# Seven products over 1280 rows, y with w1 w_out among them, in float16

## The chip, the core and the metric

The kernel runs on one core of one Trainium2 chip. The metric is the device time of one execution in microseconds (us). The median before is 390.21 us over four runs (389.89, 390.18, 390.24 and 396.35). The profile was taken on the execution of 390.18 us.

## The reference

A gated recurrence over 4 sequences of 6144 tokens with 256 channels, and then a two-layer network over all 24576 tokens, whose hidden value is the larger of two products.

```python
def _attn_ref(x, f_logit, lower_bound):          # x, f_logit: (4, 6144, 256)
    sig = 1.0 / (1.0 + np.exp(-f_logit))
    f = lower_bound + (1.0 - lower_bound) * sig
    i = 1.0 - f
    for t in range(S):
        h = f[:, t] * h + i[:, t] * x[:, t]
        y[:, t] = h
...
def _moe_ref(x, w1, w2, w_out):                  # x: (24576, 256); w1, w2: (256, 1024); w_out: (1024, 256)
    h1 = x @ w1
    h2 = x @ w2
    g = np.maximum(h1, h2)
    return g @ w_out
```

The kernel uses max(h1, h2) = h1 + relu(h2 - h1). So the output is y (w1 w_out) + relu(y (w2 - w1)) w_out: the first layer is one product, with `wd` = w2 - w1, and its output `r` is evicted through Relu; the matrix `w13` = w1 w_out (256 by 256) takes y straight to the output. Both carry the factor 1 - lower_bound, which the recurrence leaves out.

## The kernel before, in words

**Tiles.** A block is 512 tokens of one sequence (48 blocks), a pair is two blocks, `ja` and `jb` (24 pairs, numbered from 0). Channels and hidden units lie on the partitions, tokens along the free dimension. Blocks 0 to 3 are worked off by a prologue, in which also the weights are made. From pair 2 on a pair is one chunk of 1024 tokens, number c = pair + 2: its f_logit and x are cast to 16 bits into a DRAM scratch by the software queue of GpSimd (`fetch`, L96) and turned by two transposing DMAs of SyncE (`cross`, L144) into tiles `fT` and `xT`. There are two scratch tiles for each input, so GpSimd waits (`pool_waits`, L344) for the transposes of a chunk before it fetches the chunk after the next.

**Recurrence.** ScalarE makes u = sigmoid(-f) in four ACTIVATEs of a pair (`pair_gate`, L272); VectorE makes `ff` and `v` and runs four scans of 512 tokens (`pair_scans`, L285). Their outputs are the tiles `y`.

**First layer.** `first_layer(j, fc)` (L424 on) makes 128 hidden units of a block with two matmuls of 512 columns, into half of a PSUM tile `dT`. After each second call ScalarE evicts both halves through Relu into `r` (L440). There are two `dT` tiles.

**Second layer.** The hidden units of a pair of blocks are four quarters, r of `ja` and `jb` by k = 0 (the first 512) and k = 1. The output has two column halves, `lo` and `hi`. A two by two by two product by Winograd's variant of Strassen's scheme needs seven products of blocks in place of eight; the two rows are `ja` and `jb`. Its left sums S1 to S4 (`sum1` to `sum4`, L507 on) are made on VectorE for each pair, its right sums `t1` to `t4` once (`make_sevens`, L399). `sevenths(p)` (L519) lists the matmuls of one pair, each 128 by 128 by 128: a product is four token tiles times four rows of 128 hidden units. Beside the seven products stand four `linear` groups, which add y times w13 (L531): four token tiles times two channel halves each. The sums run in three PSUM banks: X is carried through five of the products, E through two and B through one. Where a partial sum is needed twice, `snapshot` copies it to SBUF (`sn`, ScalarE, L556). `leave` (L560) brings a bank out into `osb`: by a VectorE add of a snapshot (L568) or by a ScalarE copy (L566), and issues the store when a block is complete.

**The order of the work** is written out by hand (`manual_schedule`). The main loop runs over the pairs p = 2 to 23, each in 16 slots. A slot is one `first_layer` call of pair p and a sixteenth of the second layer of pair p - 1. VectorE's work for p + 1, the sums and ScalarE's gates are put at slots by the lists `seq` and `gates`. In p = 2 the slots carry the plain second layer of block 3. The last two blocks get their second layer after the loop, in plain form (`second_layer`, L461 on).

Slot s of the loop takes the entries of `seq` with a number below 9 (s + 1). Each engine works off its own instructions in the order in which they are written.

Of the kernel before, what the change touches and what calls it, by code (L numbers as in the profile page):

```python
# [10 lines left out]
BF16 = mybir.dt.bfloat16  # L11
# [7 lines left out]
def kernel(  # L19
# [19 lines left out]
    HC = 4  # L39
# [17 lines left out]
    def by_xbar(c, s):  # L57
# [13 lines left out]
    ypool = ctx.enter_context(tc.tile_pool(name="ypool", bufs=7))  # L71
    rpool = ctx.enter_context(tc.tile_pool(name="rpool", bufs=10))
# [12 lines left out]
        [dram.tile([CH, D], BF16, name=f"scr{s}{q}") for q in range(NSCR)]  # L85
# [10 lines left out]
    def fetch(c, s):  # L96
        b, t0, nt, _ = chunks[c]
        src = srcs[s][b, t0 : t0 + nt, :]
        if by_xbar(c, s):
            nc.gpsimd.dma_start(  # L100
                out=pieces(scratch[s][c % NSCR][:]), in_=pieces(src)
            )
        else:
            nat = inpool.tile([P, TB // P, D], BF16, name=("fT", "xT")[s])
            nc.gpsimd.dma_start(
                out=nat[:].rearrange("p i d -> p (i d)"),
                in_=src.rearrange("(p i) d -> p (i d)", p=P),
            )
            held[c, s] = nat
# [15 lines left out]
    def first_bf16(k, s, copy):  # L125
        raw = raws[k, s]
        nat = const.tile([P, TB // 2 // P, D], BF16, name=f"nat{k}{s}")
        copy(out=nat[:], in_=raw[:])
        raws[k, s] = nat

    def first_turn(k):
        nt = TB // 2
        for s in range(2):
            dst = ps_o.tile([P, KC, nt // P, P], BF16, name="ps")
            for q in range(nt // P):
                for h in range(KC):
                    nc.tensor.transpose(
                        dst[:, h, q, :],
                        raws[k, s][:, q, h * P : (h + 1) * P],
                        ident[:],  # L140
                    )
            raws[k, s] = dst[:].rearrange("p k i m -> p k m i")

    def cross(cs, after):  # L144
# [6 lines left out]
        for c in cs:  # L151
            for s in range(2):
                dst = inpool.tile([P, KC, CH], BF16, name=("fT", "xT")[s])
# [9 lines left out]
    def turn_steps(j):  # L163
        b, t0, nb, c, o = blocks[j]
        steps = []
        for s in range(2):
            dst = ps_o.tile([P, KC, TB], BF16, name="ps")
# [16 lines left out]
    ys = {}  # L184
    mids = {}

# [5 lines left out]
    def new_mid(key, names):  # L192
        for t in names:
            mids[key, t] = midpool.tile([P, KC, CH], BF16, name=t)
# [26 lines left out]
    def scan(j, h, ff, v, o):  # L221
        b, t0, nb, _, _ = blocks[j]
        nc.vector.tensor_tensor_scan(  # L223
            out=ys[j][:, h, :],
            data0=ff[:, h, o : o + TB],
            data1=v[:, h, o : o + TB],
            initial=0.0 if t0 == 0 else ys[j - 1][:, h, TB - 1 : TB],
# [4 lines left out]
    def scan_steps(j):  # L232
        new_mid(j, ("ff", "v"))
        u, ff, v = (mids[j, t] for t in ("u", "ff", "v"))
        ys[j] = ypool.tile([P, KC, TB], BF16, name="y")
# [7 lines left out]
    def first_recurrence(k):  # L243
        nt = TB // 2
        cols = slice(k * nt, (k + 1) * nt)
        if k == 0:
            new_mid(0, ("u", "ff", "v"))
            ys[0] = ypool.tile([P, KC, TB], BF16, name="y")
        u, ff, v, y = (*(mids[0, t] for t in ("u", "ff", "v")), ys[0])
# [6 lines left out]
        for h in range(KC):  # L256
            nc.vector.tensor_tensor_scan(
                out=y[:, h, cols],
                data0=ff[:, h, cols],
                data1=v[:, h, cols],  # L260
                initial=y[:, h, nt - 1 : nt] if k else 0.0,
# [23 lines left out]
    def pair_scans(p):  # L285
# [3 lines left out]
        for j in (2 * p, 2 * p + 1):  # L289
            ys[j] = ypool.tile([P, KC, TB], BF16, name="y")  # L290
# [19 lines left out]
    ident = const.tile([P, P], BF16)  # L310
# [3 lines left out]
    seen = const.tile([1, 16], BF16)  # L314
    waited = const.tile([P, 1], FP32)
    warm = const.tile([P, 1], FP32)
    wob = wpool.tile([P, FC, D], BF16)
    wd = wpool.tile([P, KC, DFF], BF16)
    w1T = wpool.tile([P, FC, D], BF16)
    w13 = wpool.tile([P, KC, D], BF16)  # L320
    w13d = wpool.tile([P, KC, P], BF16)
    t1 = wpool.tile([P, HC, P], BF16)
    t2 = wpool.tile([P, HC, P], BF16)
    t3 = wpool.tile([P, HC, P], BF16)
    t4 = wpool.tile([P, HC, P], BF16)
    wcd = wpool.tile([P, FC, P], BF16, name="wcd") if HC < KH else None
# [71 lines left out]

    def make_sevens():  # L399
        b11, b12 = wob[:, 0:HC, lo], wob[:, 0:HC, hi]  # L400
        b21, b22 = wob[:, KH : KH + HC, lo], wob[:, KH : KH + HC, hi]

        def minus(out, a, b):
            return lambda: nc.vector.tensor_tensor(
                out=out, in0=a, in1=b, op=ALU.subtract
            )

        steps = [
            minus(t1[:], b12, b11),
            minus(t3[:], b22, b12),  # L410
            minus(t2[:], b22, t1[:]),
            minus(t4[:], b21, t2[:]),
            minus(w13d[:], w13[:, :, lo], w13[:, :, hi]),
        ]
        if wcd is not None:
            steps.append(minus(wcd[:], wob[:, :, lo], wob[:, :, hi]))
        return steps


    rts = {}  # L420
    dts = {}

    def first_layer(j, fc):
        y = ys[j]  # L424
# [3 lines left out]
        if g == 0:  # L428
            rts[j, k] = rpool.tile([P, KH, TB], BF16, name="r")
        dT = dts["d"]  # L430
        for kc in range(KC):
# [3 lines left out]
                rhs=y[:, kc, :],  # L435
# [24 lines left out]
    def second_layer(j, slot):  # L460
        ns = TB // P  # L461
        y = ys[j]
        n = KC + FC
        total = ns * n
        for k in range(slot * total // FC, (slot + 1) * total // FC):
# [8 lines left out]
            if s < KC:  # L474
                left, right = y[:, s, i:TB:ns], w13[:, s, :]
# [23 lines left out]
    def sum_of(p, name, a, b, op):  # L499
        t = spool.tile([P, HC, TB], BF16, name="S")  # L500
# [3 lines left out]
    def quarter(p, t, k):  # L504
        return rts[2 * p + t, k][:, 0:HC, :]
# [13 lines left out]
    def sevenths(p):  # L519
# [5 lines left out]
        def product(b, left, right, fresh=False):  # L525
            n = HC
            for i in range(TB // P):
                for k in range(n):
                    steps.append([b, left, right(k), i, k, fresh and i == k == 0, None])

        def linear(b, j, cols, diff):  # L531
            y = ys[j]
            ops = [
                (y[:, kc, :].rearrange("p (m i) -> p i m", m=P), w13d[:, kc, :] if diff else w13[:, kc, cols])
                for kc in range(KC)
            ]
            for k in range(2):
                for g in range(HC, KH):
                    fc = k * KH + g
                    ops.append(  # L540
                        (
                            rts[j, k][:, g, :].rearrange("p (i m) -> p i m", m=P),
                            wcd[:, fc, :] if diff else wob[:, fc, cols],
                        )
                    )
            for i in range(TB // P):
                for a, w in ops:
                    steps.append([b, a, w, i, None, False, None])

        def then(fn):  # L550
            steps[-1][-1] = fn

# [22 lines left out]
        def sub(n):  # L575
            return lambda k: sums[p, n][:, k, :]

        def part(t, k2):
            return lambda k: rts[2 * p + t, k2][:, k, :]

        product("X", part(0, 0), lambda k: wob[:, k, lo], True)
        then(snapshot("X", 1))
        product("B", part(0, 1), lambda k: wob[:, KH + k, lo], True)
        linear("B", ja, lo, False)
        then(leave("B", ja, lo, 1, False))
        product("X", sub(2), lambda k: t2[:, k, :])
        then(snapshot("X", 2))
        product("E", sub(1), lambda k: t1[:, k, :], True)
        then(snapshot("E", 5))
        product("X", sub(3), lambda k: t3[:, k, :])  # L590
        linear("X", jb, hi, False)
        then(leave("X", jb, hi, 5, False))
        product("E", sub(4), lambda k: wob[:, KH + k, hi])
        linear("E", ja, hi, False)
        then(leave("E", ja, hi, 2, True))
        product("X", part(1, 1), lambda k: t4[:, k, :])
        linear("X", jb, lo, True)
        then(leave("X", jb, lo, None, True))

        def runner(step):  # L600
            b, left, w, i, k, fresh, after = step

            def run():
                if fresh:
                    bank[b] = ps_o.tile([P, TB // P, P], FP32, name="ps")
                if k is None:
                    a = left[:, i, :]
                else:
                    a = left(k)[:, i * P : (i + 1) * P]
                nc.tensor.matmul(  # L610
                    bank[b][:, i, :],
                    lhsT=a,
# [11 lines left out]
    with tc.manual_schedule():  # L624
# [19 lines left out]
        wt = ps_d.tile([P, 2, 2 * TB], BF16, name="dT")  # L644
# [68 lines left out]

        for p in range(PAIR0, NPAIR):
# [3 lines left out]
            if more:  # L718
                scans = pair_scans(p + 1)
                seq += [  # L720
                    (10, scans["drive0"]),
                    (44, scans["decay"]),
                    (46, scans["scan00"]),
                    (66, scans["scan01"]),
                    (76, scans["drive1"]),
                    (84, scans["scan10"]),
                    (104, scans["scan11"]),
                    (124, lambda: sum3(p)),
                ]
            if not first:  # L730
                seq += [
                    (0, lambda: sum2(p - 1)),
                    (20, lambda: sum1(p - 1)),
                    (56, lambda: sum4(p - 1)),
                ]
            seq.sort(key=lambda e: e[0])
            steps = [] if first else sevenths(p - 1)
            done_steps = 0
            gates = {2: (1, 2), 4: (1, 3), 13: (2, 0), 15: (2, 1)}
            for slot in range(2 * FC):  # L740
                first_layer(2 * p + slot // FC, slot % FC)
                if first:
                    if slot % 2 == 0:
                        second_layer(2 * p - 1, slot // 2)
                upto = (slot + 1) * len(steps) // (2 * FC)
                for step in steps[done_steps:upto]:
                    step()
                done_steps = upto
                if slot in gates:
                    q, n = gates[slot]  # L750
                    if p + q < NPAIR:
                        pair_gate(p + q, n)
                while seq and seq[0][0] < (slot + 1) * 9:
                    seq.pop(0)[1]()
                if slot == 2 and p + 3 < NPAIR:
                    c = blocks[2 * p + 6][3]
                    cross((c,), (c + 1, c + 2) if first else (c + 2,))
        for j in (NBLK - 2, NBLK - 1):
# [32 lines left out]
```

## Time and profile before

| | |
|---|---|
| profiled execution | 390.18 us, of which the program's span is 388.4 us |
| TensorE matmul (PE) | busy 370.6 us (95%), 4064 instructions seen |
| VectorE (DVE) | busy 320.8 us (83%), 383 |
| ScalarE (ACT) | busy 290.0 us (75%), 383 |
| GpSimd (POOL) | busy 50.4 us (13%), 100 |
| granted TensorE clock | 9 tenths or more in all 40 slices, 0.998 in the mean |
| chain that ended last | PE 84%, DMA 6%, DVE 4%, ACT 2% |
| DMA queues | 77.17 MB; the hardware queue of SyncE takes 61.0% of sixteen engines' span, the software queue of GpSimd 31.9% |

A group row of the page names the line, the engine, the operation, the tiles (output <- inputs), the shape and the count, then the busy time in us and the mean of one in ns, then the engine's idle time before and what ended it. Two neighbouring instructions of an engine overlap a little in the records, so a duration is longer than the time from one start to the next. Matmuls are pipelined: their row means (219 ns for 128 columns, 381 ns for 512) hold the latency too; the time that one takes from the engine is read from the distance of starts.

### The profile page before, as it was taken

How to read it: one execution, taken by the hardware profiler on the slowest of the kernel's cores; microseconds unless marked ns; L12 is line 12 of the kernel's file. 1: busy time of each engine (PE TensorE's matmuls, PEld its weight loads, DVE VectorE, ACT ScalarE, POOL GpSimd, SP SyncE). 2: the span in 40 equal slices, each digit the busy share in tenths (PEclk: the TensorE clock that was granted, in tenths of full speed). 3: DMA queues.
4: the chain of work that ended last, by engine and by line, in shares of the span. 5: the costliest groups of instructions: out<-in, count | busy, mean ns of one | idle time of the engine just before them, and what ended most of it. 6: DMA issues, size and time to landing. Idle time of an engine off the chain costs nothing.

```text
span 388.4 us, 9544 instructions
## 1 busy us (share of the span) xinstructions
PE 370.6 (95%) x4064; PEld 278.4 (72%) x4136; DVE 320.8 (83%) x383; ACT 290.0 (75%) x383; POOL 50.4 (13%) x100
## 2 busy tenths in 40 slices
PE   3999999998999999999999999999999999999995
PEld 2576667776777777777777777777777777777784
DVE  4977599995998988989989989989989889889521
ACT  3645888776788797797797787887887977977740
POOL 1500102301021021111102001202230201000000
PEclk9999999999999999999999999999999999999999
DMA  7996998989999999999999999999999994220222
GB/s 251 231 232 122 247 179 204 218 174 216 221 258 269 107 279 272 204 193 300 189 148 207 249 197 272 257 194 263 267 231 216 259 191 82 110 111 2 110 107 111
DMA packets 103389, 77.17 MB, mean 199 GB/s; under 512 B 93554, under 2 KB 94066, under 8 KB 102642
## 3 DMA queue, kind: packets, MB, share of 16 engines
q1 hardware_dynamic: 100514, 51.13, 61.0%
q0 software_dynamic: 2544, 25.17, 31.9%
q8 instruction: 32, 0.52, 0.6%
q10 hardware_dynamic: 288, 0.26, 0.2%
q14 instruction: 11, 0.09, 0.1%
HBM read 53.48 MB, written 48.23 MB: 262 GB/s over the span
## 4 chain that ended last, share of the span: by engine, by line
PE 84%; DMA 6%; DVE 4%; ACT 2%; issue 2%; SPq 1%; ACTq 0%
PE ps L610 40%; PE dT L432 35%; PE ps L479 6%; DMA fT<-scr 4%; ACT r L440 2%; DMA r<-in_moe_w_dram 2%; DVE y L223 1%; DVE S L501 1%; PE ps L373 1%; PE ps L182 1%; DVE osb L568 1%; DVE v L216 0%; ACT u L278 0%; PE ps L386 0%; SPq L117 0%
## 5 line engine op out<-in xcount | busy, mean ns | idle before, releaser
L440 ACT ACTIVATE r<-dT 128x1024 bf16<-128x1024 f32 x192 | 196.9, 1027 | 70.3 <-PE dT L432 69.4
L432 PE MATMUL dT<-y,wd 128*128 128x512 bf16 x696 | 210.7, 381 | 4.3 <-ACT r L440 2.2
L610 PEld LDWEIGHTS <-S 128*128 128x128 bf16 x1344 | 89.2, 98 | 34.7
L223 DVE TENSOR_TENSOR_SCAN y<-ff,y,v 128x512 bf16<-128x512 bf16 x88 | 112.0, 1278 | 0.8
L610 PEld LDWEIGHTS <-r 128*128 128x128 bf16 x1008 | 66.9, 98 | 27.9 <-issue 0.7
L610 PE MATMUL ps<-t,S 128*128 128x128 bf16 x1008 | 76.8, 219 | 0.5
L432 PEld LDWEIGHTS <-wd 128*128 128x128 bf16 x768 | 61.5, 98 | 11.8 <-issue 4.6
L501 DVE TENSOR_TENSOR S<-r,S 128x2048 bf16<-128x2048 bf16 x42 | 50.9, 1212 | 15.3 <-ACT r L440 15.1
L568 DVE TENSOR_TENSOR osb<-ps,sn 128x512 f32<-128x512 f32 x63 | 42.5, 675 | 23.4 <-ACT r L440 21.5
L610 PEld LDWEIGHTS <-y 128*128 128x128 bf16 x672 | 49.6, 114 | 16.4
L278 ACT ACTIVATE u<-fT 128x512 bf16<-128x512 bf16 x88 | 56.6, 644 | 3.9 <-DMA fT<-scr 3.8
L610 PE MATMUL ps<-wob,r 128*128 128x128 bf16 x672 | 51.2, 219 | 0.5
L501 DVE TENSOR_TENSOR S<-r 128x2048 bf16<-128x2048 bf16 x42 | 51.1, 1216 | 0.0
L610 PE MATMUL ps<-w,y 128*128 128x128 bf16 x504 | 48.7, 219 | 0.4
L345 POOL CAST waited<-fT 128x1 f32<-128x1 bf16 x21 | 12.7, 603 | 199.4 <-DMA fT<-scr 199.4
L556 ACT COPY sn<-ps 128x512 f32<-128x512 f32 x63 | 37.1, 589 | 0.4
L216 DVE TENSOR_TENSOR v<-u,xT 128x1024 bf16<-128x1024 bf16 x44 | 29.7, 675 | 6.7 <-ACT u L278 5.2
L610 PE MATMUL ps<-t,r 128*128 128x128 bf16 x336 | 29.0, 219 | 0.6 <-DVE osb L568 0.3
L610 PE MATMUL ps<-wob,S 128*128 128x128 bf16 x336 | 29.0, 219 | 0.2
L479 PE MATMUL ps<-wob,r 128*128 128x256 bf16 x192 | 26.2, 273 | 0.1
L206 DVE TENSOR_SCALAR ff<-u,nom 128x1024 bf16<-128x1024 bf16 (+2 forms) x54 | 22.0, 448 | 4.5 <-ACT u L200 3.9
L479 PEld LDWEIGHTS <-r 128*128 128x128 bf16 x192 | 18.8, 98 | 3.6
(53 smaller groups left out, 144.5 us busy)
## 6 DMA issues: line engine op xcount, KB each, us to landing
out_dram<-osb SPq DMA_DIRECT2D x47, 512.0 KB, 4.4
scr<-in_f_logit_dram POOLq DMA_DIRECT2D x22, 512.0 KB, 7.5
scr<-in_x_dram POOLq DMA_DIRECT2D x22, 512.0 KB, 9.8
r<-in_moe_w_dram SPq DMA_DIRECT2D x4, 512.0 KB, 7.2
fT<-in_f_logit_dram POOLq DMA_DIRECT2D x3, 256.0 KB, 8.7
xT<-in_x_dram POOLq DMA_DIRECT2D x3, 256.0 KB, 9.4
osb<-in_f_logit_dram SPq DMA_DIRECT2D x2, 256.0 KB, 3.7
osb<-in_x_dram SPq DMA_DIRECT2D x2, 256.0 KB, 3.9
```

The costliest lines, as they stand in the source:

```text
L206: nc.vector.tensor_scalar(out=ff[:, h, cols], in0=u[:, h, cols], scalar1=nom[:, h : h + 1], scalar2=1.0, op0=ALU.mult, op1=ALU.add,)
L216: nc.vector.tensor_tensor(out=like(v[:, :, cols], xT), in0=like(u[:, :, cols], xT), in1=xT, op=ALU.mult,)
L223: nc.vector.tensor_tensor_scan(out=ys[j][:, h, :], data0=ff[:, h, o : o + TB], data1=v[:, h, o : o + TB], initial=0.0 if t0 == 0 else ys[j ...
L278: nc.scalar.activation(out=mids[p + NBLK, "u"][:, h, cols], in_=held[c, 0][:, h, cols], func=AF.Sigmoid, scale=-1.0,)
L345: nc.gpsimd.tensor_copy(out=waited[:], in_=t)
L432: nc.tensor.matmul(dT[:, fc % 2, :], lhsT=wd[:, kc, fc * P : (fc + 1) * P], rhs=y[:, kc, :], start=(kc == 0), stop=(kc == KC - 1),)
L440: nc.scalar.activation(out=rts[j, k][:, g - 1 : g + 1, :].rearrange("p q (i m) -> p q i m", m=P), in_=dT[:].rearrange("p q (m i) -> p q i ...
L479: nc.tensor.matmul(ps[:, r, :], lhsT=left, rhs=right, start=(s == 0 and (r == 0 or j == NBLK - 1)), stop=(s == n - 1 and (r == 1 or j == N ...
L501: nc.vector.tensor_tensor(out=t[:], in0=a, in1=b, op=op)
L556: nc.scalar.copy(out=t[:], in_=bank[b][:])
L568: nc.vector.tensor_tensor(out=dst, in0=bank[b][:], in1=snap[name][:], op=ALU.add)
L610: nc.tensor.matmul(bank[b][:, i, :], lhsT=a, rhs=w, start=fresh, stop=after is not None, skip_group_check=True,)
```

## The change

All 16-bit tiles become float16 where they were bfloat16. The tile `y` is gone: an `r` tile gets a fifth row of 512 tokens, in which the scan writes y (channel half k beside the hidden units of half k). With that the inner dimension of each quarter is 640 rows, four rows of r and one of y, and w13 is the fifth row of the right side. The `linear` groups and `w13d` go; each product is four token tiles times five rows; the sums S run over five rows. `seed` is new: when X holds its first product, ScalarE copies bank X into bank B in PSUM, and the product of B adds to that. B then leaves by a ScalarE copy and no longer by a VectorE add. The products come in another order. The matmuls of the pairs' second layers stand in one queue, from which each slot takes 8.75 in the mean, beginning at slot 2 of p = 3; so a pair's second layer ends in slot 1 of the iteration after the next. What is left in the queue after the loop is issued before the last two blocks. The entries of `seq` and `gates` and the place of `cross` within a slot move.

```diff
-BF16 = mybir.dt.bfloat16
+HALF = mybir.dt.float16
...
-    HC = 4
+    LAG = 2
+    NSEV = 7 * 4 * 5
...
-    ypool = ctx.enter_context(tc.tile_pool(name="ypool", bufs=7))
-    rpool = ctx.enter_context(tc.tile_pool(name="rpool", bufs=10))
+    rpool = ctx.enter_context(tc.tile_pool(name="rpool", bufs=12))
...
+    def new_block(j):
+        for k in range(KC):
+            rts[j, k] = rpool.tile([P, KH + 1, TB], HALF, name="r")
+
+    def y_of(j, k):
+        return rts[j, k][:, KH, :]
...
+    def right(k, cols):
+
+        return wob[:, k * KH : (k + 1) * KH, cols], w13[:, k, cols]
...
     def sum_of(p, name, a, b, op):
-        t = spool.tile([P, HC, TB], BF16, name="S")
+        t = spool.tile([P, KH + 1, TB], HALF, name="S")
...
     def quarter(p, t, k):
-        return rts[2 * p + t, k][:, 0:HC, :]
+        return rts[2 * p + t, k][:]
...
+        def seed(b, src):
+            def go():
+                open_bank(b)
+                nc.scalar.copy(out=bank[b][:], in_=bank[src][:])
+            return go
...
-        product("X", part(0, 0), lambda k: wob[:, k, lo], True)
-        then(snapshot("X", 1))
-        product("B", part(0, 1), lambda k: wob[:, KH + k, lo], True)
-        linear("B", ja, lo, False)
-        then(leave("B", ja, lo, 1, False))
-        product("X", sub(2), lambda k: t2[:, k, :])
-        then(snapshot("X", 2))
-        product("E", sub(1), lambda k: t1[:, k, :], True)
-        then(snapshot("E", 5))
-        product("X", sub(3), lambda k: t3[:, k, :])
-        linear("X", jb, hi, False)
+        product("X", part(0, 0), plain(0, lo), True)
+        then(seed("B", "X"))
+        product("E", sub(1), given(t1), True)
+        then(snapshot("E", 5))
+        product("X", sub(2), given(t2))
+        then(snapshot("X", 2))
+        product("B", part(0, 1), plain(1, lo))
+        then(leave("B", ja, lo, None, False))
+        product("X", sub(3), given(t3))
         then(leave("X", jb, hi, 5, False))
-        product("E", sub(4), lambda k: wob[:, KH + k, hi])
-        linear("E", ja, hi, False)
+        product("E", sub(4), plain(1, hi))
         then(leave("E", ja, hi, 2, True))
-        product("X", part(1, 1), lambda k: t4[:, k, :])
-        linear("X", jb, lo, True)
+        product("X", part(1, 1), given(t4))
         then(leave("X", jb, lo, None, True))
...
-                    (10, scans["drive0"]),
-                    (44, scans["decay"]),
-                    (46, scans["scan00"]),
-                    (66, scans["scan01"]),
-                    (76, scans["drive1"]),
-                    (84, scans["scan10"]),
-                    (104, scans["scan11"]),
+                    (28, scans["drive0"]),
+                    (46, scans["decay"]),
+                    (48, scans["scan00"]),
+                    (68, scans["scan01"]),
+                    (80, scans["drive1"]),
+                    (88, scans["scan10"]),
+                    (108, scans["scan11"]),
                     (124, lambda: sum3(p)),
...
-                    (0, lambda: sum2(p - 1)),
-                    (20, lambda: sum1(p - 1)),
-                    (56, lambda: sum4(p - 1)),
+                    (9, lambda: sum1(p - 1)),
+                    (18, lambda: sum2(p - 1)),
+                    (58, lambda: sum4(p - 1)),
                 ]
+                queue += sevenths(p - 1)
...
-            gates = {2: (1, 2), 4: (1, 3), 13: (2, 0), 15: (2, 1)}
+            gates = {0: (1, 2), 2: (1, 3), 13: (2, 0), 15: (2, 1)}
...
-                upto = (slot + 1) * len(steps) // (2 * FC)
-                for step in steps[done_steps:upto]:
-                    step()
+                if p > PAIR0 + 1 or (p == PAIR0 + 1 and slot >= LAG):
+                    due += NSEV / (2 * FC)
+                    while due >= 1:
+                        due -= 1
+                        queue.pop(0)()
...
+        for step in queue:
+            step()
```

## The prediction

> **What bounds the kernel.** I cut the span into stretches of 15 us first (columns: length, then busy us and count of PE, PEld, DVE, ACT, POOL, then clock, DMA share, GB/s). From 105 to 375 us they are alike:
>
> ```profile
> 180.00:195.00 15.00, 14.84 (x178) 11.27 (x179) 13.36 (x16) 12.14 (x17) 1.90 (x4) 1.00 1.13 226
> ```
>
> PE is busy 14.84 of 15.00 us at full clock, VectorE 13.36, ScalarE 12.14. Does anything hold PE up? The chain of waits there consists of PE alone:
>
> ```profile
> 180.69 0.50 PE ps L610 x9
> 181.20 0.43 PE dT L432 x2
> 181.63 0.50 PE ps L610 x9
> ```
>
> So a slot is two wide matmuls (0.43 us, 215 ns each) and nine narrow ones (0.50 us, 56 ns each). The loop is **bound by PE's instruction count**. The list of waits shows exceptions (total, times, longest):
>
> ```profile
> ACT r L440 <- PE dT L432: 69.4, 135, 4.2
> ...
> ACT u L278 <- DMA fT<-scr: 3.8, 2, 3.0
> ...
> PE dT L432 <- ACT r L440: 2.2, 4, 1.5
> ```
>
> ScalarE has slack, but two transposes come late. The timeline has the second:
>
> ```profile
> 91.28 0.63 ACT L278 ACTIVATE u<-fT 128x512 bf16<-128x512 bf16 x1 [3.04 <-DMA fT<-scr]
> ...
> 92.87 0.59 PE L432 MATMUL dT<-y,wd 128*128 128x512 bf16 x2 [1.45 <-ACT r L440]
> ```
>
> The gate of slot 13, p = 4, stands in ScalarE's queue ahead of slot 15's relu. It waits for chunk 8, and at slot 2 of p = 5 both dT tiles are full, so PE stands until 92.87. What chunk 8 waits for is DMA work all the way back: transposes at 33.8, 53.0, 66.6 and 80.2 us, each after the fetch that GpSimd issued when the chunk before had landed. No step of that chain waits for PE. **Whatever PE gains before 92.87 is lost there.**
>
> From 92.87 to the first plain second-layer matmul at 375.34 lie 302 slots (14 of p = 5, 18 x 16): 282.47 / 302 = 0.935 us a slot, as the pieces say.
>
> **The change part by part.**
>
> *Products of 640 rows.* Before, a pair has 7 x 16 + 32 = 144 narrow matmuls (21 pairs: 3024); after, 7 x 20 = 140. A slot loses 0.25 of one: 302 x 0.25 x 56 ns = **4.2 us less**. The strided weight loads of y take 114 ns against 98; that costs nothing now, since eight matmuls on y run at the same 56 ns (slot of 88.94 us), and they become fewer (28 a pair for 32). A rule to set against this row: the Trainium skill, "TensorE: Matmul & The Clock Gate", Back-to-back issue gap, gives load-and-multiply pairs about 81 ns at 128 columns and 131 ns at 512. By it a slot would last 0.99 us and the saving be 302 x 0.25 x 81 = 6.1 us. The trace has 56 and 215 ns, so I keep 4.2.
>
> *The lag.* In p = 3 the slots 0 and 1 carry no second layer. PE stands for slot 15's relu before slot 2 then anyway (until 60.86), so nothing is gained. The 8.75 of 334 slots make 2922 of 2940; 18 matmuls come after the loop: 18 x 56 ns = **1.0 us more**.
>
> *VectorE.* The rows for its costs:
>
> ```profile
> L501 DVE TENSOR_TENSOR S<-r 128x2048 bf16<-128x2048 bf16 x42 | 51.1, 1216 | 0.0
> L568 DVE TENSOR_TENSOR osb<-ps,sn 128x512 f32<-128x512 f32 x63 | 42.5, 675 | 23.4 <-ACT r L440 21.5
> L556 ACT COPY sn<-ps 128x512 f32<-128x512 f32 x63 | 37.1, 589 | 0.4
> ```
>
> The same operation on 512 elements takes 406 ns (L404), so 512 elements more cost (1216 - 406) / 3 = 270 ns: a sum takes 1.49 us, four 1.08 us more. One add of three goes: 0.6 us less, start to start. By starts (a sum 1.13, a scan 1.13 to 1.20) a pair is about 13.1 us of VectorE before and **13.55 after, of 14.74**. That fits, but order matters. From slot 0, with 0.921 us a slot:
>
> - leave X: its last matmul (number 100, slot 13) ends about 12.65, start 12.85 (a row's 219 ns less 56 is latency); sum3 13.45 to 14.85; leave E to 15.45 = 0.7 of the next iteration;
> - sum1 waits for slot 15's relu (done 0.77): 0.8 to 2.2; sum2 to 3.6; drive0, decay, scan00 to 6.2; sum4 to 7.6; the other scans and drive1 to 11.75; then idle until 12.85.
>
> PE asks for S1 at 4.3, S2 at 6.2, S4 at 12.6, bank X at 14.6, the scans an iteration later: at least 1.0 us of slack everywhere. `make_sevens` grows by some 0.5 us at 51 us (four pieces of 128 columns, each under 284 ns, for one of 284 ns); with the longer sums the second product of p = 3 may start 0.7 us late, before the stall at 92.87, so at no cost.
>
> *ScalarE.* B's copy out is one more copy, the seed replaces a snapshot: +0.47 us a pair by starts. No row copies PSUM to PSUM. The nearest (L556) has 589 ns; below, the skill ("ScalarE: Activation LUTs", Step-by-step) calls PSUM the faster destination; above, relu of slot 5 must end before slot 8, so a seed up to 1.7 us is hidden. I take 589. Behind it stand relus, and PE waits for those; a relu may end 1.1 us late. PE needs bank B only at slot 8.9. Gates at slots 0 and 2 crowd slots 13 to 4: four relus, four gates, two copies, 6.9 of 7.7 us. Behind the DMA stall this costs, queue added up: relu 1 ends about 94.85 where PE wants 94.71, relu 3 alike: **0.2 us more**.
>
> A rule speaks against the seed: the skill's "PSUM — Partial Sum Buffer", summary, wants a ScalarE seed to be 0, any other put through PE by an identity matmul. Four of these a pair would take back all of 4.2 us (time 391.4). But the kernel issues none, and 20 matmuls last as long whether they add or overwrite; the page itself says that they add where a matmul has set the bits, and X of the pair before wrote all of that bank. Cost 0.
>
> *Queues and tiles.* SyncE's order stays store, store, fT, xT, and `cross` waits for nothing on the way. The store of jb is ready 1.8 us later in its iteration; the queue runs behind slot 2 by 16 us at chunk 9 and by nothing only at chunk 23, when transposes have 27 slots until their gate. Chunks 9 to 23 start 13.94 us apart, under the 14.74 that a pair will take. GpSimd's order stays. Copying B out on ScalarE needs a free `osb`: the latest store in question lands about 139.3 (issued 134.88, 4.4 to landing), the copy then stands at 146. The 12 r tiles are three pairs; the scan into one comes in slot 5, its last reader in slot 1. drive0 at slot 3 removes the 0.6 to 0.9 us waits for xT, which never reached PE.
>
> *float16.* No row shows it. Every engine here moves 16-bit elements; I take bfloat16's durations. Below there is nothing to gain; above see the third rival.
>
> **Sum**: 388.4 - 4.2 + 1.0 + 0.2 = 385.4 us of span; with the 1.78 us around it (390.18 - 388.4) **387.2 us**, against 390.18 for the profiled execution and 390.21 for the median, 0.8% less.
>
> **Rivals.**
> 1. *The feed takes most of it.* ScalarE's gate for chunk 16 comes at 209.68; the transpose was seen landed at 208.07. After, the gate comes about 1.7 us earlier (123 slots x 14 ns), and chunk 11 (landed 135.57 by GpSimd's record, hardly in time) 0.6. Up to 1.3 us late is hidden by the two dT tiles. If landings slip by 3 us, the gain up to there goes: 387.2 + 1.7 = 389. For it: DMA share 1.1. Against: 13.94 is under 14.74, the lead grows.
> 2. *The first stall gives way*, because chunk 8 comes as much earlier as PE does (0.7 us by slot 2 of p = 5): 386.5. Against: its chain holds no PE step.
> 3. *VectorE becomes the bound*: slower. Place: the four sums. The slack is 14.74 - 13.55 = 1.19 us, so it decides from 0.3 us a sum. The skill ("VectorE: DVE Perf Modes", What auto-detection actually checks) packs two elements a cycle when every tensor is 16 bits wide, and the row agrees (2048 / 2 / 0.96 GHz = 1067 ns, and 149 fixed). Were float16 not packed, a sum would take 2560 / 0.96 + 149 = 2.8 us, an estimate, a pair 13.55 + 4 x 1.31 = 18.8, the time 92.87 + 18.9 x 18.8 + 14 + 1.78 = 464 us. Misplaced waits of 0.2 us beyond the slack would give 387.2 + 18.9 x 0.2 = 391. Against: [...]each step of the list above has 1.0 us to spare.
> 4. The change not doing what it says (sums overwritten, not added) would show in values, not in time.
>
> **Chances.** Forecast 0.64 (386.0 to 388.3), feed 0.14, first stall 0.07, VectorE or another engine late 0.15. The range 385.8 to 390.0 leaves out the last. A measurement of this kernel tells 0.2% (0.8 us) from no change. Faster by more: forecast, first stall and half of the feed, 0.78; within 0.08; slower 0.14.
>
> **What would show it.** L603 (the narrow matmuls) 2940 less missing records; slots of 0.921 us from the restart on; restart still at about 92.9 with 3 to 5 us of ScalarE's wait before it; VectorE 13.7 of each 15 us; sums near 1490 ns, seed near 590; a group of 18 narrow matmuls before the tail. Wrong if sums exceed 1.75 us, if PE waits in each pair for a sum or a relu, or if gates wait for fT past 100 us.

## The result, and the profile after

The changed kernel takes **387.49 us** in the median of 35 runs (lowest 386.40) beside 390.3 us in 56 runs of the kernel before (lowest 389.14). Some executions of every kernel here are slow, over 1.5% above its fastest at a lower clock: these two medians count them, while all ratios, and the medians of the experiments, leave them out. The ratio is **0.9918, 95% interval 0.9897 to 0.994**: faster by 0.8%, where 387.2 us was forecast (0.8%) and the range was 385.8 to 390.0.

The profile after was taken on an execution of 393.87 us (span 391.8), in which TensorE stood once, from 216.60 on, for 4.74 us without waiting for anything that the profile shows, and then ran for a while at a clock of 0.50. Times behind that point are therefore read from a second profile of the same kernel (389.02 us, span 387.3).

A stretch of 15 us of the loop, by windows of the profile after (columns as in the prediction):

```profile
180.00:195.00 15.00, 15.00 (x177) 11.11 (x175) 13.85 (x16) 12.87 (x18) 2.91 (x5) 1.00 1.09 246
```

PE is busy without a gap at full clock. VectorE went from 13.36 to 13.85 us, ScalarE from 12.14 to 12.87. The chain of waits gives the slot (start, us, what):

```profile
106.01 0.50 PE ps L603 x9
...
109.69 0.50 PE ps L603 x9
...
113.37 0.50 PE ps L603 x9
```

Of four slots three have nine narrow matmuls and one has eight; the first of each four is shown. They come every 3.68 us: **0.920 us a slot**, where before it was 0.935. The list of waits (total, times, longest) has no new regular wait of PE:

```profile
ACT r L444 <- PE dT L436: 42.4, 79, 4.2
...
ACT u L287 <- DMA fT<-scr: 3.4, 1, 3.4
...
PE dT L436 <- ACT r L444: 2.9, 5, 1.9
...
PE ps L603 <- DVE S L504: 1.2, 1, 1.2
```

ScalarE's waits for PE fell from 135 to 79 (its slack shrank), a gate still waits once for a transpose, and PE waits once for a sum, S1 of p = 3, until 64.18. The gate and PE's restart in the timeline:

```profile
91.71 0.63 ACT L287 ACTIVATE u<-fT 128x512 f16<-128x512 f16 x1 [3.45 <-DMA fT<-scr]
...
93.30 0.59 PE L436 MATMUL dT<-r,wd 128*128 128x512 f16 x2 [1.92 <-ACT r L444]
```

Before, these lines stood at 91.28 [3.04] and 92.87 [1.45]: the same stall at the same place, with a longer wait in it. The groups of the changed operations (busy us, mean ns):

```profile
L504 DVE TENSOR_TENSOR S<-r 128x2560 f16<-128x2560 f16 x42 | 62.2, 1481 | 3.1 <-ACT r L444 3.1
...
L560 DVE TENSOR_TENSOR osb<-ps,sn 128x512 f32<-128x512 f32 x42 | 28.8, 687 | 32.7 <-ACT osb L558 23.4 <-PE ps L603 8.9 <-issue 0.2
L548 ACT COPY sn<-ps 128x512 f32<-128x512 f32 x42 | 24.7, 588 | 17.0 <-PE ps L603 16.9
...
L542 ACT COPY ps<-ps 128x512 f32<-128x512 f32 x21 | 12.1, 574 | 0.1
```

A sum over 2560 elements takes 1481 ns, and the copy from PSUM to PSUM takes 574 ns, 14 less than the copy into SBUF. The end of the loop in the second profile, in the chain of waits and in the timeline:

```profile
372.89 1.51 PE ps L603 x27
...
374.24 0.38 PE L482 MATMUL ps<-w,r 128*128 128x256 f16 x2
```

27 narrow matmuls in one piece are the nine of slot 15 and the 18 that the lag left over. The plain second layer starts at 374.24; before, its first line in the timeline was

```profile
375.34 0.38 PE L479 MATMUL ps<-w,y 128*128 128x256 bf16 x2
```

In the second profile PE restarted at 93.28 and stood once, at 271.19, for 1.73 us with no cause shown; the pair in which that fell lasted 1.90 us longer than its neighbours. From the restart to the plain second layer are 374.24 - 93.28 - 1.90 = 279.1 us. Of these 302 slots of 0.920 are 277.8 and the 18 matmuls 1.0; the 0.2 that is left lies in the first pair behind the restart. There a relu ends at 95.18, where PE wanted its tile at about 95.08 (timelines of ScalarE and of PE):

```profile
94.17 1.01 ACT L444 ACTIVATE r<-dT 128x1024 f16<-128x1024 f32 x1
...
95.23 0.59 PE L436 MATMUL dT<-r,wd 128*128 128x512 f16 x2
```

### The profile page after: what moved, and what is told of

Its sections match the earlier page's. It is cut to its first block, busy times and chain, and to the rows that moved or that the text cites. A ratio compares the mean times of both kernels' runs of the same rounds, so it can differ in the third digit from the quotient of the medians.

```text
span 391.8 us, 9417 instructions
## 1 busy us (share of the span) xinstructions
PE 372.0 (95%) x4052; PEld 273.9 (70%) x4052; DVE 329.8 (84%) x365; ACT 301.0 (77%) x404; POOL 54.0 (14%) x100
## 4 chain that ended last, share of the span: by engine, by line
PE 86%; DVE 5%; DMA 4%; issue 2%; ACT 1%; SPq 1%
PE ps L603 40%; PE dT L436 39%; PE ps L482 5%; DMA fT<-scr 3%; DVE r L232 2%; DMA r<-in_moe_w_dram 2%; ACT r L444 1%; PE ps L379 1%; DVE S L504 1%; PE ps L182 1%; DVE osb L496 0%; DVE v L225 0%; PE ps L392 0%; SPq L117 0%; DVE t L415 0%
## 5 line engine op out<-in xcount | busy, mean ns | idle before, releaser
L444 ACT ACTIVATE r<-dT 128x1024 f16<-128x1024 f32 x192 | 196.1, 1024 | 45.6 <-PE dT L436 42.4
L436 PE MATMUL dT<-r,wd 128*128 128x512 f16 x768 | 226.7, 383 | 2.9 <-ACT r L444 2.9
L603 PEld LDWEIGHTS <-S 128*128 128x128 f16 x1680 | 111.5, 101 | 46.1 <-issue 5.4
L603 PEld LDWEIGHTS <-r 128*128 128x128 f16 x1260 | 87.4, 101 | 39.4 <-issue 0.5
L232 DVE TENSOR_TENSOR_SCAN r<-ff,r,v 128x512 f16<-128x512 f16 x88 | 110.0, 1274 | 0.9
L603 PE MATMUL ps<-t,S 128*128 128x128 f16 x1260 | 98.7, 220 | 5.9 <-issue 4.7
L436 PEld LDWEIGHTS <-wd 128*128 128x128 f16 x768 | 61.6, 98 | 13.0 <-issue 4.8
L603 PE MATMUL ps<-wob,r 128*128 128x128 f16 x672 | 67.5, 219 | 0.0
L504 DVE TENSOR_TENSOR S<-r 128x2560 f16<-128x2560 f16 x42 | 62.2, 1481 | 3.1 <-ACT r L444 3.1
L504 DVE TENSOR_TENSOR S<-r,S 128x2560 f16<-128x2560 f16 x42 | 62.0, 1475 | 0.0
L482 PEld LDWEIGHTS <-r 128*128 128x128 f16 x240 | 23.9, 101 | 5.6 <-issue 0.2
```

What stands on the lines that cost most here:

```text
L232: nc.vector.tensor_tensor_scan(out=y_of(j, h), data0=ff[:, h, o : o + TB], data1=v[:, h, o : o + TB], initial=0.0 if t0 == 0 else y_of(j - ...
L436: nc.tensor.matmul(dT[:, fc % 2, :], lhsT=wd[:, kc, fc * P : (fc + 1) * P], rhs=y_of(j, kc), start=(kc == 0), stop=(kc == KC - 1),)
L444: nc.scalar.activation(out=rts[j, k][:, g - 1 : g + 1, :].rearrange("p q (i m) -> p q i m", m=P), in_=dT[:].rearrange("p q (m i) -> p q i ...
L482: nc.tensor.matmul(ps[:, r, :], lhsT=left, rhs=right, start=(s == 0 and (r == 0 or j == NBLK - 1)), stop=(s == n - 1 and (r == 1 or j == N ...
L504: nc.vector.tensor_tensor(out=t[:], in0=a, in1=b, op=op)
L603: nc.tensor.matmul(bank[b][:, i, :], lhsT=a[:, k, cols], rhs=w, start=fresh, stop=after is not None, skip_group_check=True,)
```

## The experiments

Each is an edit of the changed kernel, except the one that is headed so, which edits the kernel before. Ratios are to runs of the kernel before on the same chip; the changed kernel itself ran beside them on one of the three chips only, so a difference of a few tenths of a us between medians of two experiments says little. The changed kernel itself, unedited, ran beside the first ones:

> The changed kernel as it is, for a second profile and as the measure of the runs beside it. Theory (PE's instruction count sets the pace from the restart behind chunk 8 on): 387.2 to 387.5 us, a span near 385.5, slots of 0.921 us without a break, restart near 93 us.

It took 387.32 us, ratio 0.9901 [0.9864, 0.9939].

### The type alone

```diff
-HALF = mybir.dt.float16
+HALF = mybir.dt.bfloat16
```

> The changed kernel with bfloat16 in place of float16. Theory (no engine here is slower in one than in the other): as the changed kernel within 0.5 us, sums near 1480 ns, relus near 1025 ns. Rival (float16 costs something on an engine): a duration falls, and where it is PE's the time falls by more than 1 us.

386.9 us, ratio 0.9892 [0.9828, 0.9955]. The sums take 1482 ns, the scans 1276, relu 1024, as in float16. The type plays no part in the time that these runs could show.

### The same 38 matmuls away, early and late

```diff
             def run():
+                if p in (2, 3) and b == "B" and after is None:
+                    return
                 if fresh:
```

That is the early one; the late one has (12, 13) for (2, 3).

> The changed kernel without 19 of the 20 narrow matmuls of bank B's product in pairs 2 and 3, all of them issued before the restart near 93 us (the lo columns of the ja blocks of these two pairs then lack that product). 38 x 56 ns = 2.1 us of PE's work. Theory (the first stretch waits for chunk 8 by DMA alone): restart still at 92.9 to 93.4, time as the changed kernel within 0.5 us. Rival (the feed follows PE): restart 1 to 2 us earlier, time 1 to 2 us less.

> The same 38 matmuls left out in pairs 12 and 13, behind the restart (the lo columns of the ja blocks of these two pairs lack that product). Theory (PE's count sets the time there): 1.7 to 2.1 us less than the changed kernel, 385.3 to 385.7. Rival (VectorE or the feed is as near as PE): under 1 us less.

The late one took 385.21 us, ratio 0.9844 [0.9789, 0.9898]: 2.1 us less than the changed kernel, where 38 x 56 ns are 2.1. Behind the restart PE's work counts in full. The early one took **388.68 us**, ratio 0.9937 [0.9898, 0.9977]: not the same, but 1.4 us *more* than the changed kernel, with less to compute. Its timeline shows what the theory said, and then something that no theory had:

```profile
91.53 0.63 ACT L287 ACTIVATE u<-fT 128x512 f16<-128x512 f16 x1 [4.83 <-DMA fT<-scr]
...
93.12 0.74 PE L436 MATMUL dT<-r,wd 128*128 128x512 f16 x2 [3.30 <-ACT r L444]
...
94.51 1.06 PE L436 MATMUL dT<-r,wd 128*128 128x512 f16 x2
```

The restart has not moved (93.12); the gate waits 4.83 us for the same transpose and PE stands 3.30. But two wide matmuls then take 1.06 us where they took 0.59. The windows of 2 us give the reason in the last column but two, the granted clock:

```profile
92.00:94.00 2.00, 0.88 (x6) 0.53 (x6) 0.90 (x1) 2.00 (x4) 0.38 (x1) 0.86 1.13 364
94.00:96.00 2.00, 2.00 (x15) 1.45 (x14) 2.00 (x3) 2.00 (x5) 1.54 (x3) 0.50 1.00 285
96.00:98.00 2.00, 2.00 (x19) 1.37 (x18) 2.00 (x4) 1.50 (x3) 0.00 (x0) 0.79 2.04 424
```

The changed kernel in the second profile, in the same stretch:

```profile
94.00:96.00 2.00, 2.00 (x26) 1.42 (x24) 2.00 (x2) 2.00 (x4) 1.70 (x3) 1.00 1.04 320
```

15 matmuls against 26 in the same 2 us. (0.14 + 0.50 + 0.21) x 2 us = 1.7 us of clock are missing behind the longer stall. A pair later, slot 2 of p = 6 begins at 109.49, where in the second profile it begins at 108.19: 1.30 us later, although PE restarted 0.16 earlier. The times say the same: of the nine that the ratio counts eight have a mean clock of 0.991 to 0.996 and take 388.2 to 389.4 us; the one at 0.999 takes 387.49, as the changed kernel does. So the step "what PE gains before the restart is lost there" held, and a gain that lengthens the stall can cost more than it was.

### Gates put where they are not in a relu's way

```diff
-                    (58, lambda: sum4(p - 1)),
+                    (20, lambda: sum4(p - 1)),
...
-            gates = {0: (1, 2), 2: (1, 3), 13: (2, 0), 15: (2, 1)}
+            gates = {0: (1, 2), 2: (1, 3)}
+            if not first:
+                gates = {s: (1, s) for s in range(4)}
```

> The changed kernel with the first two gates of a pair moved from slots 13 and 15 to slots 0 and 1 of the next iteration, the other two at slots 2 and 3, and sum4 ahead of drive0 on VectorE. Theory (PE's stall at slot 2 of p = 5 comes from the relu that is queued behind the gate for chunk 8): the gate waits until 91.7 as before, but only relu 1 and later ones stand behind it; PE loses 0.8 us there where it loses 2.1 now, so about 1.3 us less, 386.0. Rival (crowding of relus and gates in slots 0 to 4 gives it back in each pair): PE waits for a relu in every pair, time 387.5 or more.

**386.02 us**, ratio 0.9894 [0.9862, 0.9926]; four of its five runs lie between 385.88 and 386.54. The fifth, which was profiled (405.39 us), met a transfer that landed 18 us late at 153.64, behind the stretch that is read here, in its timeline:

```profile
91.68 0.63 ACT L287 ACTIVATE u<-fT 128x512 f16<-128x512 f16 x1 [1.11 <-DMA fT<-scr]
...
91.72 0.59 PE L436 MATMUL dT<-r,wd 128*128 128x512 f16 x2
```

The gate waits for the same transpose, which lands at the same time. But slot 15's relu is done before it, and PE runs through: the slot that began at 93.28 in the second profile begins at 91.72, 1.56 us earlier. A pair later 1.14 of that are left (107.05 for 108.19), and 1.3 lie between the medians. What stood in the way was thus not the transfer as such but the relu queued behind the gate that waited for it. The edit also moves sum4 on VectorE, which no run separates, but the stall that is gone was ScalarE's. This version is faster than the kernel before; that it also beats the changed kernel is carried by the timeline and by four runs, for the intervals of the two ratios overlap. With the transfer 18 us late PE waited 16.76 us; what the changed kernel would have lost there no run shows.

### No lag

```diff
-    LAG = 2
+    LAG = 0
```

> The changed kernel with LAG = 0: the second layer of a pair begins in slot 0 of the next iteration. Theory (the lag puts 18 narrow matmuls behind the loop and gives nothing before the restart): up to 1.0 us less, as long as sum1, which waits for the relu of slot 15, ends before the second product asks for it; by the hand count 2.35 against 2.41 us, so 386.2 to 387. Rival (without the lag PE waits for sum1 in each pair): 0.1 to 0.3 us a pair, 388 to 392.

387.15 us, ratio 0.9924 [0.9897, 0.9951]: not told apart from the changed kernel, and not the 1.0 of 18 matmuls less. The end is as predicted: no piece of 27, and the plain second layer starts at

```profile
371.98 0.38 PE L482 MATMUL ps<-w,r 128*128 128x256 f16 x2
```

which makes slots of 0.921 us in the mean from 93.96 on. What was given back is at the start of p = 3, in the timeline:

```profile
60.99 0.59 PE L436 MATMUL dT<-r,wd 128*128 128x512 f16 x2 [0.48 <-ACT r L444]
...
63.73 0.82 PE L603 MATMUL ps<-t,S 128*128 128x128 f16 x6 [1.97 <-DVE S L504]
64.34 1.06 PE L436 MATMUL dT<-r,wd 128*128 128x512 f16 x2
```

and in the window behind it:

```profile
64.00:66.00 2.00, 2.00 (x16) 1.45 (x14) 2.00 (x4) 0.56 (x1) 0.00 (x0) 0.50 0.31 66
```

PE asks for S1 two slots sooner, stands 0.48 and 1.97 us, and works at half clock for a while. It comes to slot 2 of p = 5 at 93.96, behind the transpose, where the changed kernel begins it at 93.28 in the second profile: 0.7 us lost of the 1.0 won.

Both edits together:

> The moved gates and LAG = 0 together. Theory: both gains add where sum1 comes in time, 385.0 to 386; with the gates behind it the relu of slot 15 is no later, so sum1 isn't either. Rival: PE waits in each pair for a sum or a relu, 387.5 or more.

387.14 us in the profiled execution, ratio 0.9874 [0.9796, 0.9952], two other runs at 386.86 and 387.11 (and three at 394.5 to 399.4): more than the moved gates alone, and between the two expectations. S1 of p = 3 is 2.62 us late, and the window 64 to 66 has a clock of 0.50 again. With no stall left at the restart, what PE loses at 62 us reaches the end.

### More work for VectorE

```diff
+    junk = wpool.tile([P, KH + 1, TB], HALF, name="junk")
...
         sum_of(p, 4, quarter(p, 0, 1), sums[p, 2][:], ALU.subtract)
+        nc.vector.tensor_tensor(
+            out=junk[:, 0:5, :], in0=quarter(p, 0, 1)[:, 0:5, :],
+            in1=sums[p, 2][:, 0:5, :], op=ALU.subtract,
+        )
```

The smaller one has 3 rows in place of 5.

> The same with a sum of 1536 elements: 0.87 us more a pair by starts, 14.42 of 14.74. Theory: inside the slack, time as the changed kernel within 0.5 us. Rival (a wait of VectorE eats the slack): 1 us or more above it.

> The changed kernel with one more sum of 2560 elements a pair on VectorE, into a tile that nobody reads, right behind sum4. By starts VectorE then has 13.55 + 1.40 = 14.95 us a pair, against PE's 14.74. Theory (VectorE's slack is 1.19 us a pair): VectorE becomes the bound, slots of 0.934 us, 3 to 4 us more than the changed kernel, 390 to 391.5. Rival (VectorE is far from it): no change. Rival (it was the bound already): 20 us or more.

The smaller one: 387.39 us, ratio 0.9915 [0.9873, 0.9956]. The larger: 391.97 us, ratio 1.0036 [1.0002, 1.007]. In the larger one's timeline of VectorE, the leave of X of two pairs:

```profile
166.16 0.67 DVE L565 TENSOR_TENSOR osb<-ps,sn 128x512 f32<-128x512 f32 x1
...
181.19 0.67 DVE L565 TENSOR_TENSOR osb<-ps,sn 128x512 f32<-128x512 f32 x1
```

VectorE waits for nothing there, and a pair lasts 15.03 us where 16 slots are 14.7. The extra sum takes 1.40 us from start to start, so about 1.1 of it fitted and 0.3 stuck out. Over 18.9 pairs that is some 5.5 us; the median is 4.7 above the changed kernel's. The forecast of 3 to 4 was too low. The smaller sum's 0.87 us fits: in its trace relus of the same slot come 14.72 us apart from pair to pair, as in the changed kernel.

### Fewer matmuls in the kernel before

```diff
+            if diff:
+                ops = ops[:1]
             for i in range(TB // P):
```

> The kernel before without four of the 144 narrow matmuls of each pair (the second channel half of y in the lo columns of jb is left out), nothing else changed. Theory (the gain of the change is the count of narrow matmuls): 302 x 0.25 x 56 ns = 4.2 us less than before, 386.0; the change itself gives less by the 1.0 us of the lag. Rival (the gain comes from the other order, the sums or the lag): 0 to 2 us less than before.

Ratio 0.9869 [0.9792, 0.9947]. Three of six runs took 384.77, 385.19 and 385.19 us, 4.4 to 5.0 less than the three lowest of the kernel before beside them (389.55 to 389.75); two took 389.31 and 389.79, the first of which was profiled, and one 397.22. What four matmuls are worth in the loop is seen in that profile, away from its one disturbance. The relu of the same slot in two neighbouring pairs, in the kernel before and then here:

```profile
119.08 1.02 ACT L440 ACTIVATE r<-dT 128x1024 bf16<-128x1024 f32 x1 [0.84 <-PE dT L432]
134.02 1.02 ACT L440 ACTIVATE r<-dT 128x1024 bf16<-128x1024 f32 x1 [0.84 <-PE dT L432]
...
117.81 1.02 ACT L440 ACTIVATE r<-dT 128x1024 bf16<-128x1024 f32 x1 [0.79 <-PE dT L432]
132.53 1.02 ACT L440 ACTIVATE r<-dT 128x1024 bf16<-128x1024 f32 x1 [0.79 <-PE dT L432]
```

A pair lasts 14.94 us before and 14.72 without the four matmuls, and 14.72 is also what a pair of the changed kernel lasts (118.93 to 133.65 in the second profile). Four times 56 ns are 0.22. So the count alone gives the whole gain of a slot; the other order, the seed and the longer sums add nothing to it and take nothing from it. The disturbance, in the timeline:

```profile
183.46 1.01 PE L432 MATMUL dT<-y,wd 128*128 128x512 bf16 x2 [2.61 <-ACT r L440]
```

A gate waited for a late transpose at 180 us, PE stood 2.61 us behind its relu, and the clock of 184 to 186 us was 0.50. The mean clock of the two executions above 389 is 0.996 and 0.994, that of the three below 1.0. So the feed is near enough to be missed now and then.

### B brought out by VectorE, without the seed

```diff
-        then(seed("B", "X"))
+        then(snapshot("X", 1))
...
-        product("B", part(0, 1), plain(1, lo))
-        then(leave("B", ja, lo, None, False))
+        product("B", part(0, 1), plain(1, lo), True)
+        then(leave("B", ja, lo, 1, False))
```

> The changed kernel with bank B's old way out: X's first product copied to SBUF as a snapshot, B fresh, and added by VectorE at the exit, in place of the seed and the ScalarE copy. VectorE gets 0.60 us a pair more (14.15 of 14.74), ScalarE 0.47 less. Theory (both are inside the slack): time as the changed kernel within 0.5 us. Rival (the seed carries part of the gain): 1 us or more above it.

387.17 us, ratio 0.989 [0.9828, 0.9953]. VectorE is busy 14.57 of the 15 us from 180 on, ScalarE 12.37, PE 15.00. The seed moves some 0.6 us a pair from VectorE to ScalarE, and neither sets the pace: pairs last 14.72 us with it and without it, so it is worth nothing by itself here, and costs nothing.

## Why the prediction was right, point by point

- **PE's instruction count bounds the loop; four narrow matmuls a pair make 4.2 us.** Right. The slot fell to 0.920 us; in the kernel without lag the 302 slots behind slot 2 of p = 5 took 371.98 - 93.96 = 278.0 us, where before they took 282.47: 4.4 less. The kernel before without four matmuls has the pairs of the changed kernel, 14.72 us. The 6.1 us by the page's 81 ns would have been wrong.
- **What PE gains before the restart is lost there.** Right as to the restart: 93.30, 93.28, and 93.12 with 2.1 us of work taken away before it. That the chain does not follow PE is shown by this. What the step lacked is the clock: a stall 1.6 us longer took 1.4 us from the work behind it. The change itself lengthens the stall from 1.45 to 1.7 or 1.9 us only, and the clock stayed at 1.00. The restart was 0.4 us later than the "about 92.9" of before, in both profiles; where PE waited there at all, it restarted between 92.20 and 93.57 in the other kernels, so that is within the scatter from one execution to the next.
- **The lag costs 1.0 us.** Its size at the end is right (the piece of 27). "So nothing is gained" in p = 3 is the part that was wrong: without the lag S1 comes 2 us late there, the clock falls, and the two kernels take the same time within the noise.
- **VectorE, 13.55 of 14.74 us and 1.0 us of slack at each step.** Right. The timeline of the profile after has starts of a sum 1.40 apart and the idle stretch where it was put, ahead of the leave of X:

```profile
178.13 0.69 DVE L560 TENSOR_TENSOR osb<-ps,sn 128x512 f32<-128x512 f32 x1 [0.98 <-ACT osb L558]
178.74 1.48 DVE L504 TENSOR_TENSOR S<-r 128x2560 f16<-128x2560 f16 x1
```

  0.98 us are idle, 1.1 was worked out. The point from which the third rival decides, 0.3 us a sum, is confirmed from both sides: 0.87 us more a pair is hidden, 1.40 is not, and the larger one puts the limit at about 1.1. S1 of p = 3 was 1.18 us late in one profile and no PE wait for it shows in the other; 0.7 was forecast, and like that it came before the restart.
- **ScalarE, seed at 589 ns, hidden; 0.2 us of crowding.** Right. The seed takes 574 ns, and the pairs of the loop last 14.72 us with the seed and without it. In the first pair behind the restart the crowding shows: slot 2 of p = 6 begins 14.91 us behind slot 2 of p = 5 in the second profile (108.19 and 93.28), where pairs further on last 14.72. The relu that was forecast to end 0.14 us late, relu 1, ends 0.1 us late.
- **The rule that a seed must be 0.** The kernel issues no identity matmul for the seed, its copy is hidden, and the kernel without the seed is as fast. As a cost, 0 was right; the 391.4 us of four such matmuls did not come.
- **Queues, tiles, float16 at nothing.** Right: no gate waits for a transpose behind 100 us in either profile, and bfloat16 takes the same time.
- **The sum.** The second profile without the 1.90 us of its stall is 387.1, the medians are 387.32 and 387.49, against 387.2. An agreement to so little is in part luck: behind the restart 3.4 us went (282.47 before, 279.1 after) where 4.2 - 1.0 - 0.2 = 3.0 were forecast, and the restart's scatter of 0.4, which was in no term, made that up.

Of the rivals, the feed took nothing in the two profiled executions of the changed kernel, but one of the kernel before with fewer matmuls and one of the moved gates met it, so it is a rival to keep in mind. The first stall did not give way. VectorE did not become the bound.

## What to carry to other kernels

Where an engine's instruction count is the bound, count what an edit takes from the loop behind the last outside stall, and only there; the same work taken away ahead of the stall was worth less than nothing here. Then look at what stands in a queue between the late transfer and the bound engine: moving a waiting gate behind the relu that did not need it brought about 1.3 us, nearly half of what the whole change did. And measure the slack of the next engine by adding work to it in two sizes, one below and one above the worked-out limit: the pair says at once whether the sum of durations can be trusted.

## What the runs showed of the hardware

The granted clock fell to one half behind some PE stalls of 2 us and more. Mostly it then stayed there for about 3.4 us: the 1.7 us of clock that are missing with the early matmuls away are 3.4 us at half. All stalls of 1.45 us or more behind the first 20 us, in all profiles:

| kernel | PE stood (us) | lowest clock of a 2 us window behind it |
|---|---|---|
| before; changed, both profiles (restart) | 1.45; 1.92, 1.69 | 1.00 |
| bfloat16; late matmuls away; no seed (restart) | 1.83; 1.92; 1.91 | 1.00 |
| changed, second profile (271.19) | 1.73 | 1.00 |
| no lag (S1 of p = 3) | 0.48, then 1.97 | 0.50 |
| before with fewer matmuls (180 us) | 2.61 | 0.50 |
| moved gates, no lag (S1) | 2.62 | 0.50 |
| early matmuls away (restart) | 3.30 | 0.50 |
| changed, first profile (216.60) | 4.74 | 0.50 |
| bfloat16 (259.86) | 6.17 | 0.50 |
| moved gates, late transfer (138.47) | 16.76 | 0.50 |

The first 20 us are left out, although PE stands there for up to 3.3 us and the windows print a clock of 1.00: eight wide matmuls take 3.62 us from 12.53 on in the second profile, about twice what eight take in the loop (8 x 215 ns = 1.7), so the printed clock is not to be relied on there.

The Trainium skill, "TensorE: Matmul & The Clock Gate", Why this matters for your kernels, wants no idle gaps over about 3 us. By that the stalls of 2.0 to 2.6 us would have been free; here they were not, and the measurement decides. The length of a stall alone does not settle it, though. Without the lag PE stopped at 61.76, and the window of 62 to 64 us has a clock of 0.80, which is 0.8 us at half: the clock fell at about 63.2, only 1.4 us after PE stopped, while stalls of 1.92 us passed elsewhere. That stall had another of 0.48 us shortly before it; whether that is the reason, or the moment at which a stall begins, these runs don't tell.
